# The end of an attention stage on one core: output tiles sent in two transfers, products split by expert pairs, and one batch's output products moved to the last pair

## The chip, the cores and the metric

The kernel runs on one core of a Trainium2 chip. The metric is the device time of one execution in microseconds (us), lower is better. Engines are named as in the profile: PE (TensorE matmul), PEld (its weight loads), DVE (VectorE), ACT (ScalarE), POOL (GpSimd) and SP (SyncE, which here issues all transfers).

## The reference, cut to what matters

Three blocks run one after the other over a batch of 4 sequences of 576 positions with 512 features. The first two (a local plus pooled attention, and a token and channel mixer) are untouched by the change. The third is a causal attention with 4 experts, of which 2 are used at each position:

```python
for e in range(4):
    q, k, v = x @ wq[e], x @ wk[e], x @ wv[e]          # x: (4, 576, 512), 64 columns for each expert
    scores = where(causal, -1e9, 0.125 * (q @ k.T))
    a = softmax(scores)
    ye = a @ v @ wo[e]                                 # wo[e]: (64, 512)
    out += gate[..., e] * ye                           # gate: softmax over the 2 best experts, else 0
```

## The kernel before, in words

The last stage, from about 568 us to the end, works in eight **pairs**, numbered 0 to 7: pair i is batch b = i // 2 with two of the four experts (p = i % 2). The 576 query rows of a batch are cut into five tiles, t = 0 to 3 of 116 rows and t = 4 of 112 rows (`TQ`, `TS`). In a pair there are ten (tile, expert) items in the order t = 4, 3, 2, 0, 1 (`TORD`), two experts each.

One pair takes 14 steps, n = 0 to 13. At step n the item n is scored (`score`: PE products, a row maximum on DVE, an exponential on ACT, a scaling on DVE), and the item n - 4 (`LAG`) is transposed (`turn`: PE transposes, copies on ACT). When all items of one half s of the rows are transposed, `attend` makes the products with V (tile `o` on PE) and splits the result into a high and a low part `oh` (ACT) and `ol` (DVE), 288 columns at a time; they are kept in `ST[b]["OT"][p]` in `OB` buffers. `project_out(b, t)` multiplies them with the output weights: 3 products of 512 columns for each p, 6 in all, into one PSUM bank (`mm3`), copies the sum into a tile `y` on ACT and sends it to `out` with one transfer issued by SP. Tiles `y` and the score tiles `Pc` share one ring of 8 SBUF buffers (tag `Pc`, `PCB`), so a score tile can have to wait until an output tile has been sent.

Between the steps of a pair a list `fill` is worked off: the four Q and K projections of the next pair (`proj`, 12 products each, whose K halves are also exchanged by SP's transfers), the V projections of the next batch (`v_proj`), and the output products of a finished batch. Batch 0's and batch 1's five output products are worked off in pairs 2 and 4. Batch 2's are `held` until pair `HOLD` = 6. Batch 3's become ready only in pair 7, two tiles (t = 3, 4) when its rows' second half is attended at step 9, three (t = 2, 0, 1) after the first half at step 13.

The order of instructions on each engine is laid down when the program is built, by a scheduler that goes by program order and priorities (`ahead`). `order["on"]` chains PE instructions to the one recorded before them, so that they stay in program order; `attend` uses it.

Of the kernel before, what the change touches and what calls it, by code (L numbers as in the profile page):

```python
# [12 lines left out]
AF = mybir.ActivationFunctionType  # L13
# [4 lines left out]
DM = H * D  # L18
NP = 4
TQ = 116  # L20
NT = 5
TS = [TQ, TQ, TQ, TQ, S - 4 * TQ]
# [9 lines left out]
HS = S // 2  # L32
# [2 lines left out]
NG = NJ // JG  # L35
SLOT = 520
LAG = 4
HOLD = 6
TORD = [4, 3, 2, 0, 1]
FRONT = 3  # L40
PCB = 8
XB = 6
OB = 3
PRI = {'K': 100, 'a': 30, 'W': -60, 'S': 30}
VEC = {'k': 3, 'v': 1}
KTWICE = True
# [19 lines left out]
def body(ctx, tc, qT, kT, vw, vp, wt1, wt2, wc1, wc2, wq, wk, wvg, wo, out):  # L66
    nc = tc.nc
# [7 lines left out]
    def banks(n1, n2, stack):  # L75

        ps = pool("ps", space=bass.MemoryType.PSUM, stack=stack)

        def one(name):
            return ps.tile([128, 512], F32, tag="b1", bufs=n1, name=name)  # L80

        def two(name):
            return ps.tile([128, 2, 512], F32, tag="b2", bufs=n2, name=name)

        return one, two

    def ahead(part):

        return tc.high_priority(offset=PRI[part]) if part in PRI else nullcontext()
# [5 lines left out]
    order = {"on": False, "last": None}  # L95
# [9 lines left out]
    def mm(*a, **kw):  # L105
        behind(nc.tensor.matmul(*a, **kw))  # L106
# [45 lines left out]
    def mm3(ps, terms, first=True, last=True):  # L152
        n = 3 * len(terms)
        i = 0
        for (lh, ll), (rh, rl) in terms:
            for a, c in ((lh, rh), (lh, rl), (ll, rh)):
                mm(ps, a, c, start=first and i == 0, stop=last and i == n - 1)
                i += 1
# [54 lines left out]
    b1, b2 = banks(*ABANKS, sP)  # L213
# [249 lines left out]
    n = len(units)  # L463
# [105 lines left out]
    WQ_, WK_, WV, WO = [], [], [], []  # L569
# [29 lines left out]
    for i in range(len(seq) + 1):  # L599
# [11 lines left out]
        if len(WS) > 1:  # L611
            left = [x for x in conv if x[0] <= g + 1]
# [13 lines left out]
    b1, b2 = banks(*CBANKS, sC)  # L626
    ST = [{} for _ in range(B)]

    def split_x(b):
        xs = []  # L630
        for c in range(4):
            hi = pc.tile([128, S], F32R, tag="vh", bufs=XB, name="vh")
            lo = pc.tile([128, S], F32R, tag="vlo", bufs=XB, name="vlo")
            nc.scalar.activation(hi, U[b][:, c], AF.Copy)
            getattr(nc, XLO).tensor_tensor(lo, U[b][:, c], hi.bitcast(F32), op=OP.subtract)
            xs.append((hi, lo))
        ST[b]["xs"] = xs
        ST[b]["VV"] = pc.tile([TQ, NT, 256], F32, tag="VV", bufs=2, name="VV")
        ST[b]["L"] = pc.tile([TQ, NT, E], F32, tag="L", bufs=2, name="L")
        ST[b]["OT"] = {}  # L640
        nc.gpsimd.memset(ST[b]["L"], 0.0)

    def v_proj(b, t):

        ts = slice(t * TQ, t * TQ + TS[t])
        ps = b1("vp")
        mm3(ps[:TS[t], :260], [((x[0][:, ts], x[1][:, ts]), WV[c]) for c, x in enumerate(ST[b]["xs"])])
        nc.scalar.activation(ST[b]["VV"][:TS[t], t], ps[:TS[t], :256], AF.Copy)
        nc.vector.tensor_copy(ST[b]["L"][:TS[t], t], ps[:TS[t], 256:260])
# [31 lines left out]
    def proj(b, p, is_k, s):  # L681


        if (b, p) not in PR:
            PR[b, p] = {n: [pc.tile([128, S], F32R, tag=f"{n}{e}", bufs=2, name=f"{n}{e}") for e in range(2)]
                        for n in ("Q", "K1", "K2")}
            PR[b, p]["PT"] = [pc.tile([TQ, 3 * S], F32, tag=f"PT{e}", bufs=2, name=f"PT{e}") for e in range(2)]
        r = PR[b, p]
        w = (WK_ if is_k else WQ_)[p]
        sl = slice(s * HS, (s + 1) * HS)  # L690
        ps = b1("proj")
        mm3(ps[:, :HS], [((w[0][:, c], w[1][:, c]), (x[0][:, sl], x[1][:, sl])) for c, x in enumerate(ST[b]["xs"])])
        for e in range(2):
            A, Bh = slice(64 * e, 64 * e + 64), slice(64 - 64 * e, 128 - 64 * e)
            dst = r["K1" if is_k else "Q"][e]
            split(dst[A, sl], dst[Bh, sl], ps[A, :HS], scale=None if is_k else 0.125)
            if is_k:
                nc.sync.dma_start(r["K2"][e][Bh, sl].bitcast(F32), dst[A, sl].bitcast(F32))
                nc.sync.dma_start(r["K2"][e][A, sl].bitcast(F32), dst[Bh, sl].bitcast(F32))
# [57 lines left out]
    def attend(b, p, s):  # L757
        r = PR[b, p]
        PT = r["PT"]
        if p not in ST[b]["OT"]:  # L760
            ST[b]["OT"][p] = [pc.tile([128, S], F32R, tag=n, bufs=OB, name=n) for n in ("oh", "ol")]
        q0, q1 = s * HS, (s + 1) * HS
        o = b1("o")
        cs = [c for c in range(NT) if c * TQ < q1]
        order["on"] = True

        for c in cs:
            a = max(q0, c * TQ)
            for e in (1, 0):
                ec = (2 * p + e) * 64  # L770
                mm(o[64 * e:64 * e + 64, a - q0:q1 - q0], ST[b]["VV"][:TS[c], c, ec:ec + 64],
                                 PT[e][:TS[c], column(c, a):column(c, a) + q1 - a], start=(c == 0), stop=(c == cs[-1]))
        order["on"] = False
        oh, ol = ST[b]["OT"][p]
        split(oh[:, q0:q1], ol[:, q0:q1], o[:, :HS])

    def project_out(b, t):
        ts = slice(t * TQ, t * TQ + TS[t])
        ps = b1("wo")
        OT = ST[b]["OT"]  # L780
        mm3(ps[:TS[t]], [((OT[p][0][:, ts], OT[p][1][:, ts]), WO[p]) for p in range(2)])
        y = pc.tile([TQ, S], F32, tag="Pc", bufs=PCB, name="y")
        nc.scalar.activation(y[:TS[t], :DM], ps[:TS[t]], AF.Copy)
        nc.sync.dma_start(out[b, ts], y[:TS[t], :DM])

    pairs = [(b, p) for b in range(B) for p in range(2)]
    parts = [(k, s) for k in (True, False) for s in range(2)]
# [9 lines left out]
    fill, held, later, ready, due = [], [], [], [], []  # L797
    tiles = [(t, e) for t in TORD for e in range(2)]
    for i, (b, p) in enumerate(pairs):
        nxt = pairs[i + 1] if i + 1 < len(pairs) else None  # L800
        if nxt:
            if nxt[1] == 0:
                with ahead("x"):
                    split_x(nxt[0])
            if i or not PRE:
                fill += [lambda k=k, s=s, n=nxt: proj(*n, k, s) for k, s in parts]
            if nxt[1] == 0:
                fill += [lambda t=t, n=nxt: v_proj(n[0], t) for t in range(NT)]
                fill += [lambda n=nxt: gates(n[0])]
        steps = len(tiles) + LAG  # L810
        last = nxt is None
        if last:
            todo = {t: {s for s in range(2) if t * TQ < (s + 1) * HS and t * TQ + TS[t] > s * HS} for t in range(NT)}
        elif p == 1:
            (held if i + 2 == len(pairs) - 1 else later).extend(
                [lambda t=t, b=b: project_out(b, t) for t in range(NT)])
        wait = [{(t, e) for t, e in tiles if t * TQ < (s + 1) * HS and t * TQ + TS[t] > s * HS} for s in range(2)]
        for n in range(steps):
            now, due = due, []
            if n < len(tiles):  # L820
                with ahead("s"):
                    score(b, p, *tiles[n])
            if n >= LAG:
                with ahead("t"):
                    turn(b, p, *tiles[n - LAG])
                for s in range(2):
                    if tiles[n - LAG] in wait[s]:
                        wait[s].remove(tiles[n - LAG])
                        if not wait[s] and not last:
                            due.append((b, p, s))  # L830
                        elif not wait[s]:
                            with ahead("a"):
                                attend(b, p, s)
                            if last:
                                for t in range(NT):
                                    if s in todo[t]:
                                        todo[t].remove(s)
                                        if not todo[t]:
                                            fill.append(lambda t=t: project_out(b, t))
            if n == 1:  # L840
                fill, ready = fill + ready, []
                if i >= HOLD or last:
                    fill, held = fill + held, []
            left = max(1, steps - FRONT - n)
            for _ in range(-(-len(fill) // left)):
                with ahead("f"):
                    fill.pop(0)()
            for a in now:
                with ahead("a"):
                    attend(*a)  # L850
        ready, later = ready + later, []
# [55 lines left out]
```

## Time and profile before

| | us |
|---|---|
| median of 3 runs (770.3 to 770.59) | 770.55 |
| the profiled execution, its own time | 771.66 |
| its span in the trace | 769.9 |
| PE busy in the span | 698.3 (91%) |
| DVE, ACT, POOL busy in the span | 482.4, 397.7, 166.6 |

The time of a run covers the span and some 1.8 us around it. The shares are means over three blocks with different limits. The change touches only the stage that begins at about 568 us, so its stretches are read by themselves.

### The profile page before, as it was taken

How to read it: one execution, taken by the hardware profiler on the slowest of the kernel's cores; microseconds unless marked ns; L12 is line 12 of the kernel's file. 1: busy time of each engine (PE TensorE's matmuls, PEld its weight loads, DVE VectorE, ACT ScalarE, POOL GpSimd, SP SyncE). 2: the span in 40 equal slices, each digit the busy share in tenths (PEclk: the TensorE clock that was granted, in tenths of full speed). 3: DMA queues.
4: the chain of work that ended last, by engine and by line, in shares of the span. 5: the costliest groups of instructions: out<-in, count | busy, mean ns of one | idle time of the engine just before them, and what ended most of it. 6: DMA issues, size and time to landing. Idle time of an engine off the chain costs nothing.

```text
span 769.9 us, 15382 instructions
## 1 busy us (share of the span) xinstructions
PE 698.3 (91%) x5784; PEld 634.7 (82%) x5784; DVE 482.4 (63%) x1203; ACT 397.7 (52%) x1321; POOL 166.6 (22%) x196
## 2 busy tenths in 40 slices
PE   4177889999999999999999999999989999999973
PEld 3165667788899999999999999999988879878852
DVE  3588888456445874874585456444387766857670
ACT  5467686666543634532353234222366676767661
POOL 4387787443200311200110000000430030100000
PEclk8557979999999999999999999999999999999998
DMA  7778765332000401200020011000011021120212
GB/s 210 194 205 226 221 187 171 94 110 68 19 1 1 139 28 55 83 28 2 28 62 21 2 28 29 1 1 1 20 43 32 24 71 32 35 82 10 60 33 62
DMA packets 31587, 52.39 MB, mean 68 GB/s; under 512 B 3545, under 2 KB 16345, under 8 KB 31513
## 3 DMA queue, kind: packets, MB, share of 16 engines
q1 hardware_dynamic: 31512, 51.40, 23.4%
q8 instruction: 46, 0.75, 0.4%
q14 instruction: 29, 0.23, 0.1%
HBM read 41.95 MB, written 4.72 MB: 61 GB/s over the span
## 4 chain that ended last, share of the span: by engine, by line
PE 71%; DVE 11%; DMA 9%; ACT 4%; issue 2%; SPq 1%; ACTq 0%; DVEq 0%
PE c L106 35%; PE proj L106 7%; PE vp L106 4%; PE h L106 4%; PE s L106 3%; DMA wc_raw<-in_wc_dram 3%; PE o L106 3%; PE pu L106 3%; DMA out_dram<-y 3%; PE sl L106 2%; DMA vz<-in_vw_dram 2%; PE ol L106 2%; PE pt L109 2%; PE wo L106 2%; DVE wc_f L198 1%
## 5 line engine op out<-in xcount | busy, mean ns | idle before, releaser
L106 PE MATMUL c<-ul,wch 128*128 128x288 f32 x384 | 113.9, 297 | 1.4 <-DVE ul L532 1.4
L106 PE MATMUL c<-hh,wch 128*128 128x288 f32 x384 | 114.1, 297 | 0.5 <-DVE hl L146 0.5
L106 PE MATMUL c<-uh,wch 128*128 128x288 f32 x384 | 113.6, 296 | 0.4 <-DVE acc L555 0.4
L106 PE MATMUL c<-hl,wch 128*128 128x288 f32 x384 | 113.4, 295 | 0.0
L106 PE MATMUL c<-hh,wcl 128*128 128x288 f32 x384 | 113.3, 295 | 0.0
L106 PE MATMUL c<-uh,wcl 128*128 128x288 f32 x384 | 113.2, 295 | 0.0
L140 ACT ACTIVATE hh<-c 128x288 fp32r<-128x288 f32 x96 | 39.0, 407 | 120.7 <-PE c L106 120.7
L146 DVE SCALAR_TENSOR_TENSOR hl<-c,hh 128x288 fp32r<-128x288 f32 x96 | 43.3, 452 | 63.6 <-ACT hh L140 63.5
L106 PEld LDWEIGHTS c<-ul,wch 128*128 128x128 f32 x384 | 72.4, 189 | 2.5 <-DVE ul L532 2.2
L106 PEld LDWEIGHTS c<-hh,wch 128*128 128x128 f32 x384 | 72.2, 188 | 1.2 <-DVE hl L146 0.7
L106 PEld LDWEIGHTS c<-uh,wch 128*128 128x128 f32 x384 | 72.2, 188 | 0.9 <-DVE acc L555 0.9
L106 PEld LDWEIGHTS c<-hl,wch 128*128 128x128 f32 x384 | 72.4, 188 | 0.1
L106 PEld LDWEIGHTS c<-hh,wcl 128*128 128x128 f32 x384 | 72.4, 188 | 0.0
L106 PEld LDWEIGHTS c<-uh,wcl 128*128 128x128 f32 x384 | 72.3, 188 | 0.0
L203 POOL TENSOR_TENSOR wc_t<-wc_f,wc_t 128x512 int32<-128x512 int32 x24 | 33.3, 1390 | 169.5 <-ACT wc_t L193 156.8
L531 ACT ACTIVATE uh<-u 128x288 fp32r<-128x288 f32 x128 | 52.9, 441 | 27.5 <-PE c L106 27.5
L532 DVE TENSOR_TENSOR ul<-u,uh 128x288 fp32r<-128x288 f32 x128 | 57.0, 473 | 8.5 <-ACT uh L531 8.3
L337 ACT ACTIVATE P<-sl,nmx 128x64 f32<-128x64 f32 x160 | 48.2, 332 | 19.6 <-DVE nmx L331 19.5
L726 ACT ACTIVATE Pc<-s,nm 112x576 f32<-112x576 f32 (+4 forms) x80 | 44.4, 559 | 25.1 <-DVE nm L723 15.4
L723 DVE TENSOR_REDUCE nm<-s 112x1 f32<-112x576 f32 (+4 forms) x80 | 40.1, 514 | 9.7 <-PE s L106 8.3
L106 PE MATMUL s<-K,Q 128*112 128x288 f32 (+3 forms) x192 | 43.1, 325 | 3.0 <-DVE Q L148 1.6
L729 DVE TENSOR_SCALAR Pc<-Pc,su,gw 112x576 f32<-112x576 f32 (+4 forms) x80 | 38.4, 481 | 2.4
(168 smaller groups left out, 1782.0 us busy)
## 6 DMA issues: line engine op xcount, KB each, us to landing
wc_raw<-in_wc_dram SPq DMA_DIRECT2D x24, 512.0 KB
vp<-in_vp_dram SPq DMA_DIRECT2D x16, 336.0 KB
vz<-in_vw_dram SPq DMA_DIRECT2D x32, 160.0 KB
qT<-in_qT_dram SPq DMA_DIRECT2D x16, 288.0 KB
kz<-in_kT_dram SPq DMA_DIRECT2D x32, 144.0 KB
kT<-in_kT_dram SPq DMA_DIRECT2D x16, 288.0 KB
K<-K SPq DMA_DIRECT2D x64, 72.0 KB
out_dram<-y SPq DMA_DIRECT2D x16, 232.0 KB
```

Source lines behind the costliest of these rows:

```text
L106: behind(nc.tensor.matmul(*a, **kw))
L109: behind(nc.tensor.transpose(*a))
L140: nc.scalar.activation(hi, src, AF.Relu if relu else AF.Copy, **({"scale": scale} if scale else {}))
L146: nc.vector.scalar_tensor_tensor(lo, src, 0.0, h, op0=OP.max, op1=OP.subtract)
L198: nc.vector.scalar_tensor_tensor(f, h, -0x40000000, a, op0=OP.bitwise_and, op1=OP.bitwise_or)
L203: nc.gpsimd.tensor_tensor(flat(dst, shape).bitcast(I32), f, t.bitcast(I32), op=OP.add)
L337: nc.scalar.activation(P[:, t, h], sv[:, bk, i], AF.Exp, bias=nmx[:, bk, i:i + 1], scale=0.125, accum_out=sm[:, t, h:h + 1])
L531: nc.scalar.activation(hi, u, AF.Copy)
L532: getattr(nc, ULO).tensor_tensor(lo, u, hi.bitcast(F32), op=OP.subtract)
L723: nc.vector.tensor_reduce(nm[:nq], sv, axis=AX.X if t < 4 else AX.XY, op=OP.max, negate=True)
L726: nc.scalar.activation(pv_, sv, AF.Exp, bias=nm[:nq], accum_out=su[:nq])
L729: nc.vector.tensor_scalar(P[:nq, :n], P[:nq, :n], su[:nq], ST[b]["W"][:nq, t, 2 * p + e:2 * p + e + 1], op0=OP.mult, op1=OP.mult)
```

## The change

Output tiles are sent as two transfers, rows 0 to 111 and rows 112 to 115 (one where the tile has 112 rows). Batch 2's output products go to pair 7 in place of pair 6 (`HOLD` 7), for which one more buffer for each of `oh` and `ol` is kept (`OB` 4); the space comes from a smaller reserve for transfers that GpSimd would issue. In pair 7 at most one entry of `fill` is worked off at steps 2, 4, 6 and at each step from 8 on. A new function `out_first` makes the p = 0 products of batch 3's tiles 0 and 1 ahead of time into the two-bank PSUM tile. Batch 3's output tiles are queued in the order 2, 3, 4, 0, 1, with their p = 1 products chained in program order, and their copies are halved: 288 columns on ACT, 224 on DVE.

```diff
-HOLD = 6
+HOLD = 7
-OB = 3
+OB = 4
@@
-    def project_out(b, t):
-        ts = slice(t * TQ, t * TQ + TS[t])
-        ps = b1("wo")
+    part = {}
+
+    def out_first(b, tiles):
+
+        ps = b2("wo")
+        for k, t in enumerate(tiles):
+            ts = slice(t * TQ, t * TQ + TS[t])
+            oh, ol = ST[b]["OT"][0]
+            part[b, t] = ps[:TS[t], k]
+            mm3(part[b, t], [((oh[:, ts], ol[:, ts]), WO[0])], last=False)
+
+    def project_out(b, t, late=False):
+        n = TS[t]
+        ts = slice(t * TQ, t * TQ + n)
+        begun = (b, t) in part
+        ps = part.pop((b, t)) if begun else b1("wo")[:n]
         OT = ST[b]["OT"]
-        mm3(ps[:TS[t]], [((OT[p][0][:, ts], OT[p][1][:, ts]), WO[p]) for p in range(2)])
+        for p in range(1 if begun else 0, 2):
+            order["on"] = late and p == 1
+            mm3(ps, [((OT[p][0][:, ts], OT[p][1][:, ts]), WO[p])], first=p == 0, last=p == 1)
+        order["on"] = False
         y = pc.tile([TQ, S], F32, tag="Pc", bufs=PCB, name="y")
-        nc.scalar.activation(y[:TS[t], :DM], ps[:TS[t]], AF.Copy)
-        nc.sync.dma_start(out[b, ts], y[:TS[t], :DM])
+        if late:
+            nc.scalar.activation(y[:n, :HS], ps[:, :HS], AF.Copy)
+            nc.vector.tensor_copy(y[:n, HS:DM], ps[:, HS:])
+        else:
+            nc.scalar.activation(y[:n, :DM], ps, AF.Copy)
+
+        for a0, a1 in ((0, 112), (112, n)):
+            if a0 < a1:
+                nc.sync.dma_start(out[b, t * TQ + a0:t * TQ + a1], y[a0:a1, :DM])
@@
-                                for t in range(NT):
+                                for t in (2, 3, 4, 0, 1):
                                     if s in todo[t]:
                                         todo[t].remove(s)
                                         if not todo[t]:
-                                            fill.append(lambda t=t: project_out(b, t))
+                                            fill.append(lambda t=t: project_out(b, t, late=True))
+            if last and n == 4:
+                fill.append(lambda: out_first(b, (0, 1)))
@@
-            for _ in range(-(-len(fill) // left)):
+            for _ in range(-(-len(fill) // left) if not last else int(n % 2 == 0 or n >= 8) * min(1, len(fill))):
@@
-    nc = bacc.Bacc("TRN2", target_bir_lowering=False, num_devices=1)
+    nc = bacc.Bacc("TRN2", target_bir_lowering=False, num_devices=1, dynamic_dma_scratch_size=1024)
```

## Rows read from the trace of the kernel before

**Rows 1.** Chain that ended last, 752 us to the end: start us, us, what

```profile
754.42 3.91 PE wo L106 x16
...
759.44 0.49 ACT y L783
```

**Rows 2.** SP's waits, 759 us to the end: us, times, longest us

```profile
SPq L903 <- DMA out_dram<-y: 8.5, 1, 8.5
```

**Rows 3.** Windows at the end, at a K exchange: busy by engine, clock, DMA share, GB/s

```profile
755.00:755.50 0.50, 0.50 (x4) 0.39 (x3) 0.37 (x1) 0.00 (x0) 0.00 (x0) 1.00 0.89 217
755.50:756.00 0.50, 0.50 (x4) 0.39 (x3) 0.00 (x0) 0.00 (x0) 0.00 (x0) 1.00 0.77 254
756.00:756.50 0.50, 0.50 (x4) 0.39 (x3) 0.00 (x0) 0.00 (x0) 0.00 (x0) 1.00 0.31 119
...
759.60:768.50 8.90, 0.00 (x0) 0.00 (x0) 0.00 (x0) 0.33 (x1) 0.00 (x0) 0.71 0.24 80
768.50:769.90 1.40, 0.00 (x0) 0.00 (x0) 0.00 (x0) 0.00 (x0) 0.00 (x0) 0.50 0.00 0
638.30:639.00 0.70, 0.70 (x7) 0.59 (x6) 0.04 (x1) 0.29 (x1) 0.00 (x0) 1.00 0.41 105
```

**Rows 4.** SP in order of time: two of the last outputs, two K exchanges

```profile
753.04 0.32 SPq L784 DMA_DIRECT2D out_dram<-y  x1
...
759.96 0.31 SPq L784 DMA_DIRECT2D out_dram<-y  x1
...
637.33 0.47 SPq L699 DMA_DIRECT2D K<-K  x1
637.90 0.54 SPq L698 DMA_DIRECT2D K<-K  x1
```

**Rows 5.** Windows by pair: length, busy of PE, PEld, DVE, ACT, POOL, clock, DMA

```profile
609.61:635.87 26.26, 24.41 (x176) 20.81 (x178) 16.91 (x51) 19.09 (x55) 5.78 (x4) 1.00 0.23 69
635.87:660.74 24.87, 24.42 (x206) 22.59 (x208) 18.99 (x69) 16.28 (x52) 0.00 (x0) 1.00 0.10 25
660.74:685.82 25.08, 23.64 (x168) 19.98 (x169) 16.87 (x50) 17.27 (x51) 2.81 (x2) 1.00 0.26 72
...
711.73:736.76 25.03, 22.87 (x162) 19.18 (x163) 16.16 (x50) 16.09 (x49) 0.00 (x0) 1.00 0.25 72
736.76:753.32 16.56, 13.16 (x99) 9.88 (x99) 10.05 (x38) 10.70 (x38) 0.00 (x0) 1.00 0.01 2
753.32:758.78 5.46, 5.46 (x30) 3.89 (x30) 0.46 (x1) 0.83 (x2) 0.00 (x0) 1.00 0.31 85
```

**Rows 6.** ACT's waits, 600 to 760 us: us, times, longest us

```profile
ACT Pc L726 <- DMA out_dram<-y: 9.4, 8, 1.7
```

**Rows 7.** Window in pair 2 ahead of its first output transfer, columns as in the pairs

```profile
616.00:621.75 5.75, 5.19 (x36) 4.47 (x35) 4.21 (x12) 5.65 (x16) 5.38 (x4) 1.00 0.12 28
```

**Rows 8.** Engines in order of time, 746 to 760 us

```profile
753.32 1.11 PE L106 MATMUL o<-PT,VV 116*64 116x288 f32 x12 [1.00 <-ACT PT L751]
...
754.47 0.41 ACT L140 ACTIVATE oh<-o 128x288 fp32r<-128x288 f32 x1 [1.21 <-PE o L106]
...
754.91 0.46 DVE L150 TENSOR_TENSOR ol<-o,oh 128x288 fp32r<-128x288 f32 x1 [5.21 <-ACT oh L140]
...
757.93 0.85 PE L106 MATMUL wo<-wo_hi,ol 128*116 128x512 f32 x3
758.36 1.57 ACT L783 ACTIVATE y<-wo 116x512 f32<-116x512 f32 x3 [3.48 <-PE wo L106]
```

**Rows 9.** Groups of instructions, 711.73 to 736.76 us: count, busy us, mean ns

```profile
L783 ACT ACTIVATE y<-wo 116x512 f32<-116x512 f32 (+1 forms) x5 | 3.0, 597 | 0.5 <-PE wo L106 0.5
```

**Rows 10.** Queues of the whole span: packets, MB, share of 16 engines

```profile
q1 hardware_dynamic: 31512, 51.40, 23.4%
```

**Rows 11.** Windows at the stage's start, columns as in the pairs

```profile
570.00:572.00 2.00, 0.63 (x3) 0.39 (x3) 1.90 (x6) 2.00 (x6) 2.00 (x2) 1.00 0.00 0
572.00:574.00 2.00, 1.57 (x8) 1.55 (x9) 1.90 (x6) 1.98 (x8) 2.00 (x2) 0.56 0.00 0
```

## Prediction, made before the changed kernel was run

> **What bounds the kernel now.** I read the chain that ended last first, then SP's waits behind it. The last products with the output weights run on PE (16 in 3.91 us, so 0.244 us each), three copies `y` follow on ACT, and the last of them ends at 759.44 + 0.49 = 759.93 [rows 1]. No engine computes after that, but the span ends at 769.9: SP waits 8.5 us for the output transfers [rows 2], and the bytes flow until about 768.5 [rows 3]. So the first 10 us to look at are a drain.
>
> The windows say what kind of drain. From 759.6 to 768.5 the 16 transfer engines are busy with a share of 0.24 at 80 GB/s, as if four of sixteen worked. All three tiles sent there have 116 rows. The tile with 112 rows, issued at 753.04 [rows 4], drives the share to 0.89 and 0.77 at 217 and 254 GB/s; by 756.0 to 756.5 it is back at 0.31 [rows 3]. The reader is to see that one tile size uses about a quarter of the engines and the other nearly all.
>
> Next the windows by pair, each from the last `attend` of the pair before to its own. PE idles 0.45 us in pair 3 (24.87 less 24.42), which sends nothing, but 1.85 and 1.44 us in the pairs with output tiles, 2 and 4 [rows 5]. ACT waits 9.4 us, in 8 pieces, for output tiles to leave the ring shared with the score tiles [rows 6]. So the slow transfers also reach back into PE. Last, from 711.73 to 758.78 (from the last `attend` of pair 5 to the last product), PE works 22.87 + 13.16 + 5.46 = 41.49 of 47.05 us [rows 5]: 5.56 us idle, 3.40 of them in the 16.56 us window of pair 7, which has hardly any fill.
>
> **The change, part by part.**
>
> *Sending 112 and 4 rows: the drain.* Before, the bytes end about 8.5 us after the last `y`. For a 112-row transfer I have the one issued at 753.04: its burst is over at about 756.1, so 3.1 us, with a 116-row transfer beside it [rows 3, 4]. A K exchange of 72 KB, issued at 637.33, has moved its bytes by 639.0, in 1.67 us [rows 3, 4]; the remaining 152 KB of a tile at 254 GB/s make it 2.3. Alone I expect 2.8, nearer to the row of the same size. The rest of four rows is issued behind it; two K issues follow each other after 0.57 us [rows 4], and 8 KB need less time than the tile's 224, so it adds nothing as long as the large part is in flight. If nothing covers it, it adds 0.6. Three tiles, issued some 0.7 us apart, are 672 KB, at 217 to 254 GB/s 2.7 to 3.1 us; starting 1.5 us ahead of the last `y` plus the delay, they end within the same bounds, at worst at 4.3. Drain: 8.5 - 2.8 = **5.7 us** less (4.2 to 6.2).
>
> Here two rules of the Trainium skill stand against each other. The row says 0.24 of the engines for 116 rows and up to 0.89 for 112 [rows 3]. The page DMA: Bandwidth & Descriptors, section Rules for kernel authors, says that splitting a transfer by partitions isn't worth it, because both parts go over the same 16 engines; by that the drain would keep its 8.5 us and the sum would lose this part and the next but one. The same page, section Why a DMA increments its semaphore by 16 and not by 1, says that the engines used are the largest number up to 16 that divides the slowest dimension: 4 for 116 rows, 16 for 112. The trace sides with the second.
>
> *Halved last copies.* The three `y` copies run one behind the other on ACT, 1.57 us, and end 1.15 us after the last product (757.93 + 0.85 = 758.78) [rows 8]. After, each tile's products end some 0.7 us apart (three products), and a half copy takes about what a split of 288 columns takes, 0.41 on ACT and 0.46 on DVE [rows 8]. So the last copy ends 0.5 us after the last product: **0.65 us** less (0.4 to 0.75).
>
> *Sending 112 and 4 rows: the ring in pairs 2 and 4.* With about 3 us from issue to landing, a tile frees its ring place before the ring of 8 comes round, at two allocations in a step of some 2 us. PE's idle time over pair 3's is 1.40 and 0.99; of the 1.40, 0.56 fall from 616 to 621.75, ahead of the first output transfer [rows 5, 7]. That leaves 0.84 + 0.99 = 1.8; I take **1.7 us** less (0.9 to 1.9).
>
> *Batch 2's products in pair 7, and the p = 0 products ahead.* These move 30 products (30 x 0.244 = 7.3 us) from pair 6 to pair 7, and 6 (1.5 us) from the tail to before it. PE's work stays the same, so only its idle time counts, 5.56 now. Pair 7 gets fill at every second step. But pair 6 loses it: its four projections are worked off in steps 0 to 3, and from there to step 1 of pair 7 nothing fills the gaps. Its PE work falls to 22.87 - 7.3 = 15.6, below DVE's 16.16; ACT's falls to 16.09 - 3.0 = 13.1, with the five `y` copies gone [rows 5, 9]. So the thin stretch is moved rather than removed. Priced at pair 7's idle share (3.40 of 16.56, of which 1.0 is the wait for the last transposed tile [rows 5, 8]), some 14 us without fill idle about 2.2; the last wait stays with 1.0, two waits at the half's products 0.9, the rest 0.2: 4.3. Gain 5.56 - 4.3 = **1.3 us** (from -1.0, with pair 6 and 7 as thin as pair 7 was, 6.6, to 3.7, with only the waits at the halves left, 1.9). After the last `attend`, 3 + 9 products remain in place of 18; the first three cover the split of 0.41 + 0.46 us [rows 8] but for some 0.15.
>
> *At nothing.* 16 more issues on SP, each 0.3 us [rows 4]: SP waits for `y` between them, and K exchanges come ahead of the outputs in `fill`; uncovered, only those behind the last `y` count, and they are in the drain. The fourth `oh`/`ol` buffer removes a wait that the held tiles would cause, and adds none. The smaller reserve serves transfers issued by GpSimd; the page's queues show none [rows 10]. The chain on the late products keeps the order that the program has.
>
> **Sum.** 5.7 + 0.65 + 1.7 + 1.3 = 9.35 us. From the profiled span, 769.9, that gives 760.55, from its own time, 771.66, 762.3; the median lies 1.1 below that time, so 770.55 - 9.35 = **761.2 us**.
>
> **Rivals.**
> - *The thin stretch eats more* (idle time grows in pair 6, DVE leading): for it speak DVE's 16.16 us of work against PE's 15.6; against it, that pair 7 alone managed 16.56 us with 10.05 of DVE and less order among its steps. With idle 6.6 or more and the slower ends of drain and ring: 763.5 to 766.5.
> - *The fill closes nearly all gaps*: idle 1.9, and drain 6.0: 758.5. Against it speaks that pair 6 has only four projections.
> - *The split does not spread the transfer*: drain and ring keep their price, and 770.55 - 0.65 - 1.3 = 768.6; with 0.6 for each later issue it reaches 769 and more. The 112-row window speaks against it. The section Rules for kernel authors, named above, would have it so.
> - *Slower: the granted clock falls.* Where PE idled 1.37 of 2 us at the stage's start, the clock went from 1.00 to 0.56, its lower level of 1.2 GHz for most of the stretch [rows 11]. If the thin stretch in pair 6 does the same, PE's products take twice as long there. One such stretch of 4 us at 0.57 costs 1.7 us; it ends slower than before only from 9.35 us of added time, some 19 us at the lower level with PE as the bound. Pair 7's 21 us of PE work, all at 1.2 GHz, would give about 782. Against it: pair 7 idled 3.40 of 16.56 us in pieces and kept 1.00 [rows 5]. The page TensorE: Matmul & The Clock Gate, section A second HAM failure mode: psum-queue depth-cycling, tells of just such small idle times between groups driving the clock up and down; no row of this stage shows it.
>
> **How the numbers follow.** The forecast, 758.6 to 763.4 by the terms' usual bounds, has 0.78; the thin stretch 0.09; the closed gaps 0.08; no spreading 0.03; the clock 0.02. Within 0.2% (769.0 to 772.1), about what a measurement of this kernel can tell from no change, lies some of the third rival: 0.02. Slower 0.02, faster 0.96. The range that leaves out no more than two in ten goes from 758.2 to 764.4, since the cost of the thin stretch and the landing of a lone 112-row transfer are bounded, not shown.
>
> **What would show it.** The windows after the last `y` at a share well over 0.5 and SP's last wait near 3 us show the drain right; a share of 0.25 shows it wrong. No wait of ACT for `out_dram` in pairs 2 and 4, and PE idle there near 0.5 to 1.0, show the ring right. PE busy in the windows of pairs 6 and 7 shows the fourth term: some 4 us idle in all, most of it in pair 6. The last copy ending 0.5 us after the last product shows the second. What would make the prediction wrong is above all the order that the scheduler gives PE in pair 7: late transposes behind held products, with ACT waiting for them.

## The result

The changed kernel takes 760.72 us (median of 6, 757.88 to 762.51), the kernel before 770.67 in the same session (770.3 to 771.07): a ratio of 0.9868, 95% interval 0.9848 to 0.9887, 9.95 us less. The forecast was 761.2 us, with 758.2 to 764.4 as the range. The profiled execution took 759.61 us, with a span of 757.8.

Part of the differences between kernels lies ahead of the changed stage. The first `attend` of pair 0 begins at 579.67 us in the kernel before and at 578.08 in the changed one, and over the twelve executions profiled here it fell anywhere from 575.59 to 581.35. So besides the times I use the length of the last stage, from that `attend` to the end of the span: it is the part that the change touches. The pairs without output tiles (1, 3 and 5) keep within 0.05 us of 24.86 in all twelve; the whole stage repeats less well where tiles wait for the ring, as the first experiment shows. Before: 769.9 - 579.67 = 190.23. After: 757.8 - 578.08 = 179.72, so 10.51 us less.

First the marks, from the engines in order of time, PE alone: the first `attend` in the kernel before, then the first and the last in the changed kernel.

```profile
579.67 2.25 PE L106 MATMUL o<-PT,VV 116*64 116x288 f32 x20
```

```profile
578.08 2.25 PE L106 MATMUL o<-PT,VV 116*64 116x288 f32 x20
...
748.42 1.11 PE L106 MATMUL o<-PT,VV 116*64 116x288 f32 x12 [0.55 <-ACT PT L751]
```

The windows of the changed kernel by pair, with the columns of [rows 5]: pairs 2, 4, 6, 7, then the last `attend` to the last product, then three windows from the end of the last copy.

```profile
607.93:633.35 25.42, 24.41 (x175) 20.80 (x175) 17.21 (x51) 19.20 (x56) 5.78 (x4) 1.00 0.25 71
...
658.22:683.10 24.88, 24.43 (x176) 20.81 (x175) 17.60 (x51) 18.37 (x54) 2.80 (x2) 1.00 0.26 73
...
707.96:726.49 18.53, 16.36 (x133) 13.96 (x132) 15.38 (x50) 12.98 (x45) 0.00 (x0) 1.00 0.13 32
726.49:748.42 21.93, 20.82 (x134) 16.21 (x134) 11.27 (x40) 13.68 (x43) 0.00 (x0) 1.00 0.20 60
748.42:753.66 5.24, 4.32 (x24) 2.75 (x24) 1.36 (x4) 1.24 (x3) 0.00 (x0) 1.00 0.36 113
...
754.53:755.20 0.67, 0.00 (x0) 0.00 (x0) 0.00 (x1) 0.00 (x0) 0.00 (x0) 1.00 0.30 113
755.20:756.40 1.20, 0.00 (x0) 0.00 (x0) 0.00 (x0) 0.00 (x0) 0.00 (x0) 0.64 0.64 198
756.40:757.80 1.40, 0.00 (x0) 0.00 (x0) 0.00 (x0) 0.00 (x0) 0.00 (x0) 0.50 0.00 0
```

The reader is to see four things. The last copy ends at 754.53 and the bytes are gone about 1.9 us later, where [rows 2, 3] had 8.5. Over these 1.9 us the share is 0.30 and then 0.64, in the mean 0.52, not "well over 0.5" as the prediction's sign had it: by the rows some 310 KB are still to move, little more than the last tile's 232. Pairs 2 and 4 idle 1.01 and 0.45 us on PE, where [rows 5] had 1.85 and 1.44; between 590 and 757 us ACT's waits no longer contain an output transfer. Pair 6 is 18.53 us long and pair 7 21.93, 40.46 together, where before it was 753.32 - 711.65 = 41.67. And between the last `attend` and the last product PE idles 0.92 us, where before it had none [rows 5]. SP's last wait tells the drain in one line:

```profile
SPq L928 <- DMA out_dram<-y: 1.5, 1, 1.5
```

The tail of the changed kernel, engines in order of time, shows two waits that the prediction did not have:

```profile
751.82 0.41 ACT L800 ACTIVATE y<-wo 116x288 f32<-116x288 f32 x1 [0.23 <-PE wo L106]
...
752.26 0.39 DVE L801 COPY y<-wo 116x224 f32<-116x224 f32 x1 [0.25 <-ACT y L800]
...
752.71 0.49 PE L106 MATMUL wo<-wo_hi,oh 128*116 128x512 f32 x1 [0.92 <-DVE y L801]
...
753.27 0.39 PE L106 MATMUL wo<-wo_hi,ol 128*116 128x512 f32 x1
753.70 0.41 ACT L800 ACTIVATE y<-wo 116x288 f32<-116x288 f32 x1 [1.47 <-PE wo L106]
754.14 0.39 DVE L801 COPY y<-wo 116x224 f32<-116x224 f32 x1 [1.49 <-ACT y L800]
```

The DVE half of a copy does not run beside the ACT half but begins when it ends: at the last tile the ACT half ends at 753.70 + 0.41 = 754.11, and the DVE half begins at 754.14. And the last three products, of the second tile begun ahead, wait for the copy of the first one in the other bank.

From the stage's 10.51 us: pairs 2 and 4 give 0.84 and 1.23 (26.26 to 25.42, and 26.11 to 24.88 from `attend` to `attend`), pairs 6 and 7 together 1.21, and the way from the last `attend` to the end, called the tail from here on, 7.20 (16.58 to 9.38). The 7.20 are 0.22 of products (5.46 to 5.24), 0.28 of copies (1.15 to 0.87) and 6.7 of drain. What these parts are due to is for the experiments.

### The profile page after: what moved, and what is told of

It reads as the page before. It is cut to its first block, busy times and chain, and to the rows that moved or that the text cites. A ratio compares the mean times of both kernels' runs of the same rounds, so it can differ in the third digit from the quotient of the medians.

```text
span 757.8 us, 15395 instructions
## 1 busy us (share of the span) xinstructions
PE 695.4 (92%) x5784; PEld 632.5 (83%) x5784; DVE 484.2 (64%) x1208; ACT 398.3 (53%) x1321; POOL 164.2 (22%) x196
## 4 chain that ended last, share of the span: by engine, by line
PE 75%; DVE 10%; DMA 8%; ACT 4%; issue 2%; POOL 1%; SPq 1%; ACTq 0%; DVEq 0%; POOLq 0%
PE c L106 35%; PE proj L106 6%; DMA wc_raw<-in_wc_dram 4%; PE s L106 4%; PE vp L106 4%; PE wo L106 4%; PE h L106 4%; PE o L106 3%; PE pu L106 3%; PE sl L106 3%; PE pt L109 3%; DMA wt_raw<-in_wt_dram 2%; PE ol L106 2%; DMA qT<-in_qT_dram 1%; PE pod L106 1%
## 5 line engine op out<-in xcount | busy, mean ns | idle before, releaser
L723 DVE TENSOR_REDUCE nm<-s 112x1 f32<-112x576 f32 (+4 forms) x80 | 40.5, 514 | 12.2 <-PE s L106 10.5
```

What stands on the lines that cost most here:

```text
L723: nc.vector.tensor_reduce(nm[:nq], sv, axis=AX.X if t < 4 else AX.XY, op=OP.max, negate=True)
```

## The experiments

My theory at this point: the split of the transfers carries the drain and the ring; holding batch 2's products only moves idle time. The rival: the order of the work at the end, with products held and begun ahead, carries several us.

**The smaller reserve alone**, on the kernel before:

```diff
-    nc = bacc.Bacc("TRN2", target_bir_lowering=False, num_devices=1)
+    nc = bacc.Bacc("TRN2", target_bir_lowering=False, num_devices=1, dynamic_dma_scratch_size=1024)
```

> The kernel before with nothing but the smaller reserve for GpSimd's transfers. Six runs of the changed kernel spread from 757.88 to 762.51 us where six of the kernel before kept within 0.8 us, and its profiled execution reached the last stage 1.6 us earlier. My theory: the reserve has no part in the gain, so 770.3 to 771.1 us with the old narrow spread, and the wider spread comes from elsewhere. Rival: shifted SBUF addresses change the loads of the first block; then the spread of some 4 us shows here too, and the median lies up to 2 us under 770.7.

771.12 us (12 runs, 767.63 to 774.71) against 771.41 (17 runs, 768.64 to 773.13): ratio 1.0, interval 0.9984 to 1.0016. The reserve has no part in the gain, within 1.2 us either way. A scatter of 7 us shows in this kernel, where I expected the old narrow one, but in the kernel before in the same session there is one of 4.5 us too; so the 0.8 us of the first session are not the kernel's usual scatter, and nothing is left that speaks for the rival.

The two profiles also tell what a stage's length is worth. The stage is 190.84 us long here and 190.23 in the kernel before, 0.61 apart. Of this, 0.46 us are in pair 6, where ACT waits 4.3 us for output tiles to leave the ring and in the kernel before 3.8. So a stage with such waits is not known to better than some 0.6 us. The tails, 16.60 and 16.58 us, agree.

**The split alone**, on the kernel before:

```diff
-        nc.sync.dma_start(out[b, ts], y[:TS[t], :DM])
+        for a0, a1 in ((0, 112), (112, TS[t])):
+            if a0 < a1:
+                nc.sync.dma_start(out[b, t * TQ + a0:t * TQ + a1], y[a0:a1, :DM])
```

> The kernel before with nothing but the split of each output tile into 112 and 4 rows. My theory: this edit carries most of the gain, the drain (6.5 us by the traces) and the waits for the ring in pairs 2, 4 and also 6 (2 to 3 us), so 761.2 to 762.6 us, a drain of about 2 us after the last copy and no wait of ACT for output transfers. Rival: the order of the work at the end carries it; then the time stays above 766 us.

760.77 us (4 runs), ratio 0.9858 (0.9846 to 0.9871): the time of the whole change. Its windows, pair 6, pair 7, last `attend` to last product, last copy to the last bytes:

```profile
708.13:731.72 23.59, 22.69 (x163) 19.21 (x162) 16.86 (x50) 16.45 (x50) 0.00 (x0) 1.00 0.27 77
731.72:748.28 16.56, 13.30 (x99) 9.91 (x99) 9.71 (x38) 10.81 (x38) 0.00 (x0) 1.00 0.01 1
748.28:753.77 5.49, 5.48 (x30) 3.90 (x30) 0.46 (x1) 0.84 (x2) 0.00 (x0) 1.00 0.28 85
754.92:757.90 2.98, 0.00 (x0) 0.00 (x0) 0.00 (x0) 0.00 (x0) 0.00 (x0) 1.00 0.73 228
```

Three tiles whose copies come close together go out in 2.98 us at a share of 0.73 and 228 GB/s, where [rows 3] had 0.24 and 80. Pair 6, which still sends batch 2's tiles, shrinks from 25.11 to 23.59 without any product moved. The stage is 181.14 us long, 9.09 of the 10.51 us less.

**The change without the split**, whole tiles in one transfer:

```diff
-        for a0, a1 in ((0, 112), (112, n)):
-            if a0 < a1:
-                nc.sync.dma_start(out[b, t * TQ + a0:t * TQ + a1], y[a0:a1, :DM])
+        nc.sync.dma_start(out[b, ts], y[:n, :DM])
```

> The changed kernel with whole tiles of 116 rows sent in one transfer. My theory: the drain goes back to about 8.5 us behind the last copy with a DMA share near 0.25, and the ring's waits come back in pairs 2 and 4 and now fall into pair 7 with its ten output tiles: 6.5 + 2.0 + up to 3 us over the changed kernel, 769 to 772 us. Rival: the four transfer engines are no limit where the products are spread out in time; then the drain is under 6 us and the time under 767.

766.16 us (5 runs), ratio 0.9939; the stage is 186.74 us long, 7.02 more than in the changed kernel and 3.49 less than before. The time misses the expectation of 769 to 772. SP's last wait, ACT's wait for the ring, and the windows of pair 7 and of the drain:

```profile
SPq L926 <- DMA out_dram<-y: 7.0, 1, 7.0
```

```profile
ACT Pc L726 <- DMA out_dram<-y: 5.6, 5, 1.4
```

```profile
727.41:749.32 21.91, 20.81 (x135) 16.22 (x135) 11.24 (x40) 13.66 (x43) 0.00 (x0) 1.00 0.19 57
...
755.43:762.40 6.97, 0.00 (x0) 0.00 (x0) 0.00 (x1) 0.00 (x0) 0.00 (x0) 0.67 0.24 90
```

Pairs 2 and 4 are as long as before (26.29 and 26.06), so the ring's waits are theirs, as expected. In pair 7 the waits I expected do not come: 21.91 us with whole tiles, 21.93 with split ones. And the drain is 7 us rather than 8.5, since two of the three tiles were issued 2.5 and 1.9 us ahead of the last copy's end. The time, 766.16, is under the rival's 767, but its drain of under 6 us did not come, and the share is 0.24 again, as of four engines: the rival's cause is not the right one.

Everything but the split takes 3.49 us off the stage by itself, the split alone 9.09; together they take 10.51, so 2.07 us of what they remove is the same time. Most of it lies in pairs 6 and 7: from 41.67 us the whole tiles come to 40.44, the split alone to 40.15, both to 40.46.

**Products back in pair 6**, all else as changed:

```diff
-HOLD = 7
+HOLD = 6
```

> The changed kernel with batch 2's output products back in pair 6, all else as changed. My theory: PE's idle time only moves between pairs 6 and 7, so holding them gains about 1 us: 761 to 763 us, pair 6 close to 25 us again and pair 7 close to 17, with 4 to 5.5 us of idle PE in both together. Rival: holding them is worth the 3 us or more that pair 7 idled before; then 763.5 us or more.

759.31 us (4 runs, 757.88 to 762.16), not to be told from 760.72 by the times; the stage is 179.05 us long, 0.67 less than with the products held. Pairs 6 and 7:

```profile
711.22:734.81 23.59, 22.69 (x163) 19.22 (x163) 16.86 (x50) 16.42 (x50) 0.00 (x0) 1.00 0.27 76
734.81:750.97 16.16, 14.04 (x105) 10.94 (x105) 10.34 (x40) 10.43 (x38) 0.00 (x0) 1.00 0.01 2
```

They idle 0.90 and 2.12 us on PE; with the products held it was 2.17 and 1.11. So holding moves idle time from pair 7 to pair 6 and gains nothing; in this kernel it loses 0.7 us. I had expected it to gain 1. That is beyond the scatter: pairs 6 and 7 together take 39.75 us here, 39.93 and 39.95 in the two later kernels with `HOLD` 6, and 40.43 to 40.65 in the six with `HOLD` 7. Of the 0.71 us, 0.26 are idle time of PE; the rest is in its busy time, and why that is longer is open.

**A cut at 113 rows**, for batch 3's tiles:

```diff
-        for a0, a1 in ((0, 112), (112, n)):
+        cut = min(n, 113) if late else 112
+        for a0, a1 in ((0, cut), (cut, n)):
```

> The changed kernel with batch 3's four tiles of 116 rows sent as 113 and 3 rows, all else as changed; the order of the work is the same. My theory: the number of transfer engines is the largest number up to 16 that divides the rows, so one engine for 113 rows: a DMA share of about 0.06 and some 25 GB/s after the last copy, 3 times 226 KB in a drain of 25 to 30 us, and 780 to 788 us. Rival: what counts is only that most rows go in one large transfer of a size near 112; then the share stays over 0.6, the drain near 2 us and the time near 760.

789.46 us in one run, where the kernel before took 769.66 beside it, and the stage is 209.74 us long; both the time and the drain, some 32 us behind the last copy, are a little over what I expected (780 to 788, 25 to 30). Two windows of the drain:

```profile
760.00:765.00 5.00, 0.00 (x0) 0.00 (x0) 0.00 (x0) 0.00 (x0) 0.00 (x0) 0.50 0.07 25
765.00:775.00 10.00, 0.00 (x0) 0.00 (x0) 0.00 (x0) 0.00 (x0) 0.00 (x0) 0.50 0.07 26
```

One row more than 112, and the share is that of one engine in sixteen, at 26 GB/s. Here too each tile goes out as a large transfer and a small one, so neither two transfers nor the large one's size make the gain, but its number of rows. The Trainium skill has it that the engines used are the largest number up to 16 that divides the rows (DMA: Bandwidth & Descriptors, Why a DMA increments its semaphore by 16 and not by 1): 1 for 113, 4 for 116, 16 for 112. The trace agrees at all three: shares of 0.07, 0.24 and, with the gaps between tiles, 0.73. These three counts do not tell that rule from another that gives the same numbers, the greatest common divisor of the rows and 16.

**Two PSUM tiles for the products begun ahead**:

```diff
-        ps = b2("wo")
         for k, t in enumerate(tiles):
...
-            part[b, t] = ps[:TS[t], k]
+            part[b, t] = b2("wo")[:TS[t], 0] if k else b1("wo")[:TS[t]]
```

> The changed kernel with the early p = 0 products of tiles 0 and 1 in two separate PSUM tiles, where the changed kernel has them in the two banks of one. In the changed kernel the last three products wait 0.92 us for the copy of the other bank. My theory: the wait is for the tile and not for the bank, so it goes: products end about 1 us earlier, and from the last first-half attend to the end of the span it is 8.3 to 8.7 us in place of 9.38. Rival: the wait is for something else, such as the split of the low part; then 9.4 us stay.

758.16 us (4 runs; the kernel before took 769.66 beside it, ratio 0.9852, 0.9833 to 0.987). The tail is 8.85 us in place of 9.38, where I expected 8.3 to 8.7, and the stage 179.15. In order of time:

```profile
750.66 0.40 PE L106 MATMUL wo<-wo_hi,oh 128*116 128x512 f32 x1
...
750.86 0.41 ACT L799 ACTIVATE y<-wo 116x288 f32<-116x288 f32 x1 [0.23 <-PE wo L106]
...
751.12 0.40 PE L106 MATMUL wo<-wo_hi,ol 128*116 128x512 f32 x1
```

The last three products now begin ahead of the copy they had waited for. In both kernels the two tiles lie in different banks; what changed is that they are two tiles to the program, so the wait was for the tile and not for the bank. PE needs 4.07 us from the last `attend` to the last product and idles none. Of the 1.17 us that this saves (5.24 less 4.07), 0.64 are taken back behind the last copy, so the tail is 0.53 shorter. The three tiles now follow each other so closely that the transfers set the end:

```profile
752.39:754.80 2.41, 0.00 (x0) 0.00 (x0) 0.00 (x0) 0.00 (x0) 0.00 (x0) 0.91 0.74 240
```

**Whole copies on ACT** for batch 3's tiles:

```diff
-        if late:
-            nc.scalar.activation(y[:n, :HS], ps[:, :HS], AF.Copy)
-            nc.vector.tensor_copy(y[:n, HS:DM], ps[:, HS:])
-        else:
+        if True:
             nc.scalar.activation(y[:n, :DM], ps, AF.Copy)
```

> The changed kernel with batch 3's output tiles copied whole on ACT, all else as changed. In the changed kernel the DVE half of a copy starts when the ACT half ends (0.41 and 0.39 us, 0.83 in all). My theory: two halves of one bank run one behind the other, so a whole copy at 0.6 us is faster: 0.2 us less at the last tile and 0.2 less in the wait of the last products, 8.9 to 9.1 us from the last first-half attend to the end in place of 9.38. Rival: ACT gets crowded by three whole copies and the tail grows past 9.5.

758.2 us (4 runs, ratio to the kernel before 0.9865), the stage 179.81, and the tail 9.28 us, where I expected 8.9 to 9.1.

```profile
750.19 0.49 PE L106 MATMUL wo<-wo_hi,oh 128*116 128x512 f32 x1 [0.69 <-ACT y L800]
```

```profile
751.19 0.60 ACT L800 ACTIVATE y<-wo 116x512 f32<-116x512 f32 x1 [1.05 <-PE wo L106]
```

A whole copy takes 0.60 us where two halves took 0.83, and PE's wait falls from 0.92 to 0.69, both as expected. But between the end of the last copy and the end of the span it takes 3.61 us against 3.27, and pairs 6 and 7 are 0.19 longer, so nothing is left of it. Why that last stretch grew I did not test. What is shown: halving a copy between ACT and DVE gains nothing here.

**Both, with the products back in pair 6** (`HOLD` 6, the two PSUM tiles, whole copies, those of tiles 0 and 3 on DVE):

```diff
-HOLD = 7
+HOLD = 6
...
-        if late:
-            nc.scalar.activation(y[:n, :HS], ps[:, :HS], AF.Copy)
-            nc.vector.tensor_copy(y[:n, HS:DM], ps[:, HS:])
+        if late and t in (0, 3):
+            nc.vector.tensor_copy(y[:n, :DM], ps)
```

> The changed kernel with batch 2's output products back in pair 6, the early products in two separate PSUM tiles, and batch 3's tiles copied whole, tiles 0 and 3 on DVE, the others on ACT. My theory: the stage is shorter by 0.7 us for pairs 6 and 7, as with the products back in pair 6 alone, and by 1.0 to 1.5 in the tail: from the first attend of pair 0 to the end of the span 177.3 to 178.2 us, against 179.7 of the changed kernel and 190.2 of the kernel before; the time 758 to 759.5. Rival: the scheduler lays the order differently and takes back what the tail gains; then 179 us or more.

758.87 us (4 runs, ratio to the kernel before 0.9861, so by the times not to be told from the two kernels ahead of it); the stage is 178.59 us long, the tail 8.78. That is 1.13 us less than the changed kernel by the stage, but 0.4 over the upper end of what I expected. As with the two tiles, three tiles follow each other closely, and their transfers are the end now: in the 2.66 us behind the last copy the share is 0.68, at 215 GB/s.

**Without the remaining four rows** of batch 3's tiles:

```diff
-        for a0, a1 in ((0, 112), (112, n)):
+        for a0, a1 in ((0, 112), (112, 112 if late else n)):
```

> The changed kernel without the transfers of rows 112 to 115 of batch 3's tiles (these rows are left out of the output); the order on PE, DVE, ACT and POOL is the same. My theory, as predicted: the four remaining rows land in the shadow of the 112, so from the first attend of pair 0 to the end of the span it stays at 179.4 to 179.8 us (179.72 in the changed kernel). Rival: each of the added transfers has a fixed price of its own behind the large one; then the stage is 0.5 us shorter or more.

This kernel leaves the four rows out of the output. Its stage is 759.0 - 579.36 = 179.64 us long against 179.72, its tail 9.34 against 9.38 (one run). The four rows cost nothing that shows.

**The remaining rows issued by ACT**, on the shortest version:

```diff
-                nc.sync.dma_start(out[b, t * TQ + a0:t * TQ + a1], y[a0:a1, :DM])
+                q = nc.scalar if late and a0 else nc.sync
+                q.dma_start(out[b, t * TQ + a0:t * TQ + a1], y[a0:a1, :DM])
```

> The shortest version so far (products back in pair 6, two PSUM tiles, whole copies) with batch 3's remaining four rows issued by ACT in place of SP. My theory: the drain is now three tiles of 232 KB at some 240 GB/s behind the first of the last three copies, so the issuing engine changes little: 178.2 to 178.8 us from the first attend of pair 0 to the end (178.59 with SP). Rival: SP's issue time of 0.35 us for each transfer delays the large ones; then 177.9 us or less. A third: the issues on ACT hold up its last copy; then over 179.

759.3 us (5 runs), ratio to the kernel before 0.985 (0.9823 to 0.9877); the stage is 178.51 us long against 178.59. SP's issue time for the four rows does not set the end.

All runs by the stage's marks, in us:

| kernel | span | first `attend` | stage | pairs 6 and 7 | last `attend` to end |
|---|---|---|---|---|---|
| before | 769.9 | 579.67 | 190.23 | 41.67 | 16.58 |
| reserve alone | 770.5 | 579.66 | 190.84 | 42.11 | 16.60 |
| split alone | 759.4 | 578.26 | 181.14 | 40.15 | 11.12 |
| change, whole tiles | 763.7 | 576.96 | 186.74 | 40.44 | 14.38 |
| the change | 757.8 | 578.08 | 179.72 | 40.46 | 9.38 |
| change, `HOLD` 6 | 760.4 | 581.35 | 179.05 | 39.75 | 9.43 |
| change, cut at 113 | 787.7 | 577.96 | 209.74 | 40.43 | 39.42 |
| change, two PSUM tiles | 756.3 | 577.15 | 179.15 | 40.43 | 8.85 |
| change, whole copies | 755.4 | 575.59 | 179.81 | 40.65 | 9.28 |
| both, `HOLD` 6 | 757.9 | 579.31 | 178.59 | 39.93 | 8.78 |
| change, four rows left out | 759.0 | 579.36 | 179.64 | 40.44 | 9.34 |
| both, rows issued by ACT | 756.7 | 578.19 | 178.51 | 39.95 | 8.70 |

## Why the prediction was right

*The drain* was the largest term, 5.7 us within 4.2 to 6.2. The mechanism is shown by the split alone and by the cut at 113 rows. The size was 6.7, above the upper bound; this term was mis-sized. The 2.8 us taken for the new drain are near the 2.98 of the split alone, where three copies end close together; in the changed kernel the last products come later by the wait of 0.92 us, the first two tiles are nearly gone by then, and 1.9 us remain.

*The copies*, 0.65 within 0.4 to 0.75, gave 0.28, below the lower bound. The step that failed: "a half copy takes about what a split of 288 columns takes". Each half does (0.41 and 0.39), but they run one behind the other; the prediction took it that they run together. What makes them take turns was not tried: they share the PSUM bank, the tile `wo` and the tile `y`.

*The ring in pairs 2 and 4*, 1.7 within 0.9 to 1.9, gave 2.07, a little above the upper bound. The mechanism holds: with whole tiles the two pairs are back at their old length. The window of pair 4 in [rows 5] ends at 685.82, 1 us ahead of its last `attend` at 686.78; the pair was 26.11 us long. PE's idle time over the full pair is 1.43, as good as the 1.44 read, so the forecast was not off by that; but PE's busy time in the pair also falls, from 24.68 to 24.43, and a sum of idle time leaves that out.

*Batch 2's products in pair 7*, 1.3 us. The idle time left was put at 4.3 us, and it is 2.17 + 1.11 + 0.92 = 4.20; the total of the term, from the last `attend` of pair 5 to the last product, is (758.78 - 711.65) - (753.66 - 707.96) = 1.43. But the cause was put wrongly. The term's 5.56 us of idle time held pair 6's own waits for the ring, which the prediction counted in pairs 2 and 4 only. Of the 9.4 us of [rows 6], pair 2 has 2.2, pair 4 has 3.4, and pair 6 the most:

```profile
ACT Pc L726 <- DMA out_dram<-y: 3.8, 3, 1.7
```

The split removes them by itself, 25.11 to 23.59, 1.52 us with no product moved. With them gone, holding the products is worth less than nothing, 0.67 us more. Without the split it would have looked right: the change with whole tiles takes 1.23 us less in pairs 6 and 7, and ACT waits for no output tile there. "The thin stretch is moved rather than removed" was right to the end; I should have drawn from it that nothing remains to gain. That the term's number came out, 1.43 for 1.3, is luck. The rest that the change has over the split alone, 1.42 us, lies in the tail (11.12 to 9.38), with the products begun ahead and the output tiles finished one by one; pairs 6 and 7 take 0.31 back. Which of those two edits carries the tail was not separated.

*At nothing* stood the added issues, the four rows, the reserve and the buffer; the runs agree on the rows and the reserve, and on the issues as far as the last four-row transfers go. The fourth buffer was not run by itself.

The sum was 9.35 us, the stage gave 10.51 and the medians 9.95. Three of the four terms lie outside the bounds I gave them, the drain 1.0 and the ring 0.4 us over what I took, the copies 0.4 under, and the fourth lies inside with a wrong cause. The main mechanism was right; that the time came within 0.5 us of the forecast, with single runs that scatter by several us, is in part luck. Of the rivals none came: the split spreads the transfers, the granted clock stayed at 1.00 through pairs 6 and 7, and the thin stretch idles 2.17 us in pair 6, close to the 2.2 of the estimate.

## What to carry to other kernels

Look at the share of the transfer engines in a drain before looking at its bytes: for tiles of nearly the same size it was 0.24 at 116 rows, 0.07 at 113 and 0.73 at 112. One line that cuts the rows at a multiple of 16 took 9.1 us off the stage by itself, where the whole change took 10.5. When several edits promise to remove the same idle time, give each wait to one edit only: pair 6's waits went to the wrong one here, and the edit that seemed to earn them costs time. Two parts of one on-chip tile can be one thing to the program's waits: a product waited 0.92 us for the copy of another bank until the tile was made two. And two engines on halves of one copy need not run side by side: here they took turns, 0.41 and 0.39 us, where one engine took 0.60 for the whole.

## What was not expected of the hardware

The times of one and the same program can scatter by little in one session and by much in another: the kernel before by 0.8 us and by 4.5. The start of the last stage moves as much between kernels: the first `attend` lay between 575.59 and 581.35 us over the twelve profiled ones, whose edits lie behind it but for the reserve and the buffers, while the pairs 1, 3 and 5 behind it were each within 0.05 us of 24.86. No program was profiled twice, so that its own scatter lies ahead of the stage is likely but not shown. A difference of one us in a late stage is better read from that stage's own marks than from the times, and where transfers hold up the work even these differed by 0.6 us.
